# Depthwise convolution of the large groups in 64x64 tiles of TensorE, its output written to DRAM in parts of 48 and 10 partitions

## The chip, the cores and the metric

One core of one Trainium2 chip. The time is the device time of one execution in microseconds (us), lower is better. A run that is compared with the kernel before shares its chip and its rounds with it.

## The reference

The kernel computes a causal depthwise convolution of seven taps over x (8 sequences x 4160 tokens x 192 channels; the taps are a softmax of a weight for each of 8 heads, 24 channels per head), and then a channel mix on its result y:

```python
out = np.einsum('hk,bskhg->bshg', w, x_unf)          # y: 7 taps, 8 heads of 24 channels
xk = mu_k * x + (1.0 - mu_k) * x_prev                # x is now y, x_prev is y one token earlier
xr = mu_r * x + (1.0 - mu_r) * x_prev
k = np.maximum(xk @ w_k, 0.0)                        # 192 -> 1024
v = k * k @ w_v                                      # 1024 -> 192
r = 1.0 / (1.0 + np.exp(-(xr @ w_r)))                # 192 -> 192
return (r * v).astype(np.float32)
```

## The kernel before

The sequences are done in four pairs. TensorE works in bundles: four matmul sections K (`k_mm`, 64 rows x 128 columns of weights, two row halves at a time), one section r of the same shape, one section V of full 128x128 shape, and in most bundles one *unit* of convolution for tokens that are needed later. The convolution is a matmul with a banded Toeplitz matrix per head, `toe`: 128 rows of x (six of them halo) give 120 tokens of y. x is loaded in groups of up to ten such blocks. The first four groups are small and are transposed on TensorE; the large ones (10 and 9 blocks in the first pair, then 10, 10, 10, 5 per pair) are written to DRAM as y and read back by a transposing transfer into yT.

```python
    def conv_mm(g, c):                         # a unit: two chunks, one bank of PSUM each
        ...
        ps2 = ring.tile([P, 2, BANK], FP32, tag="k", name="ps_c")
        for k, hs in enumerate(chunks(g)[c : c + 2]):
            w = G * len(hs)
            ps = ps2[:, k, 0 : nb * 2 * w].rearrange("p (n s c) -> p n s c", n=nb, s=2)
            conv_ps[g, c + k] = ps
            for i, h in enumerate(hs):
                nc.tensor.matmul(out=ps[:, :, :, i * G : (i + 1) * G], lhsT=toe[:, h, :],
                    rhs=xbs[g][:, :nb, :, h * G : (h + 1) * G], start=True, stop=True)
    ...
    def y_write(g):
        ...
        nc.sync.dma_start(
            out=y_drams[p][blk0 * BLK : (blk0 + nb) * BLK, :].rearrange("(n t) c -> t n c", t=BLK),
            in_=ys[g][:BLK, :nb, :])
    ...
    def conv(g, c):
        ...
        conv_mm(g, c)                          # four or two matmuls, then their copies
        for k in range(c, min(c + 2, len(chunks(g)))):
            conv_out(g, k, nc.scalar.copy)
    ...
        for b in range(quads[-1][2] + 1):      # one bundle (cut): K, r, V, then convolution
            k_section(part); k_relu(n); run(rq, b); run(vq, b); run(mixes, b)
            k_square(n); run(vo, b); run(xt, b); run(late, b)
```

PSUM is a ring of four tiles of two banks each; K, r, V, the convolution and the transposes take turns in it. ScalarE does the relus, the sigmoids and the copies of the convolution. VectorE does the squares, the mixes and the final products.

## Time and profile before

| | before |
|---|---|
| median of 4 runs | 436.25 us (436.14 to 436.48) |
| TensorE busy | 421.9 us of 434.0 (97%) |
| bundle with one large unit / without | 6.344 us / 5.937 us |
| from the K section of the second bundle to that of the eighth, six bundles (18.03 to 62.04 us) | 44.01 us |

The bundle lengths are differences of the start times of K sections in the trace; they repeat to 0.001 us through most of the run. The stretch from 18 to 62 us is called the *start stretch* below; it holds the fourth group, then four bundles with the first pair's large groups, two units to a bundle, and one bundle with a single unit.

### The profile page before, as it was taken

To read this page: it belongs to the slowest core of one execution; us is meant where nothing else is said; L and a number is where in the kernel's file an instruction comes from. 1 tells how busy PE (TensorE), PEld (TensorE's weight loads), DVE (VectorE), ACT (ScalarE), POOL (GpSimd) and SP (SyncE) were. 2 spreads that over 40 slices of the span, in tenths; PEclk is the share of its full clock that TensorE was granted. 3 is DMA by queue.
4 is the path that set the end of the run, shared out by engine and by line. 5 is a ranking of instruction groups with operands and counts; after the bars stand their busy time and mean duration, and the time that the engine had idled before them with its cause. 6 is when DMAs were issued, how large, how long until landed. Compare 5 with 4: busy or idle time off the path is not lost.

```text
span 434.0 us, 11361 instructions
## 1 busy us (share of the span) xinstructions
PE 421.9 (97%) x4709; PEld 294.6 (68%) x4709; DVE 380.3 (88%) x678; ACT 349.2 (80%) x474; POOL 48.4 (11%) x73
## 2 busy tenths in 40 slices
PE   8789999999999999999999999999999999999995
PEld 3465767766866776677677667766766776667785
DVE  6879889998988989889888998898898898999983
ACT  5788988888897788889888888888898788777780
POOL 7450001202300000202110100102000000000000
PEclk9999999999999999999999999999999999999999
DMA  8998766999797953869598982696744463621223
GB/s 134 191 153 142 191 174 121 209 200 181 172 170 212 182 149 98 130 178 196 162 167 179 186 170 75 138 227 131 178 118 130 121 159 117 114 68 46 74 74 110
DMA packets 134484, 64.30 MB, mean 148 GB/s; under 512 B 85132, under 2 KB 134048, under 8 KB 134432
## 3 DMA queue, kind: packets, MB, share of 16 engines
q1 hardware_dynamic: 96050, 48.31, 44.8%
q0 software_dynamic: 37488, 14.66, 29.3%
q8 instruction: 37, 0.61, 0.6%
q10 hardware_dynamic: 894, 0.61, 0.5%
q14 instruction: 15, 0.12, 0.1%
HBM read 29.92 MB, written 36.99 MB: 154 GB/s over the span
## 4 chain that ended last, share of the span: by engine, by line
PE 89%; ACT 3%; DVE 3%; DMA 2%; issue 1%; POOL 1%; ACTq 0%
PE ps_v L515 41%; PE ps_k L458 37%; PE ps_r L532 7%; PE ps_c L285 4%; DMA wk<-in_moe_w_k_dram 2%; ACT k_sb L487 2%; ACT y L324 1%; DVE k L501 1%; DVE yT L367 0%; POOL xb L125 0%; PE ps_t L358 0%; DVE xr L434 0%; DVE d L411 0%; DVE xk L438 0%; DVE xk L434 0%
## 5 line engine op out<-in xcount | busy, mean ns | idle before, releaser
L487 ACT ACTIVATE k_sb<-ps_k 128x1024 bf16<-128x1024 f32 x260 | 246.6, 1053 | 25.6 <-PE ps_k L458 25.0
L515 PE MATMUL ps_v<-wv,k 128*128 128x192 bf16 x2080 | 182.7, 246 | 1.3 <-ACT k_sb L487 1.3
L458 PE MATMUL ps_k<-xk,wk 64*128 64x512 bf16 (+1 forms) x1632 | 180.9, 367 | 1.9 <-DVE xk L438 1.0
L515 PEld LDWEIGHTS <-k 128*128 128x128 bf16 x2080 | 168.7, 98 | 11.3 <-issue 11.3
L501 DVE TENSOR_TENSOR k<-k_sb 128x1024 bf16<-128x1024 bf16 x260 | 168.0, 687 | 0.4 <-ACT k_sb L487 0.2
L458 PEld LDWEIGHTS <-wk 64*128 64x128 bf16 x1632 | 74.7, 94 | 97.1 <-issue 19.0
L556 DVE TENSOR_TENSOR o_sb<-ps_v,r_sb 128x768 f32<-128x768 f32 x64 | 61.2, 957 | 35.3 <-PE ps_v L515 33.4
L324 ACT CAST y<-ps_c 120x480 bf16<-120x480 f32 (+4 forms) x134 | 54.3, 483 | 43.7 <-PE ps_c L285 43.7
L540 ACT ACTIVATE r_sb<-ps_r 128x768 bf16<-128x768 f32 x65 | 56.4, 867 | 1.3 <-PE ps_r L532 1.3
L125 POOL DMA_DIRECT2D xb<-in_x_dram x34 | 30.8, 910 | 210.5 <-PE ps_k L458 164.6
L532 PEld LDWEIGHTS <-xr 64*128 64x128 bf16 x780 | 34.1, 94 | 16.8 <-issue 1.4
L532 PE MATMUL ps_r<-wr,xr 64*128 64x192 bf16 x780 | 42.9, 243 | 1.6 <-DVE xb L105 0.8
L434 DVE TENSOR_SCALAR xk<-d,mu 128x512 bf16<-128x512 bf16 (+1 forms) x99 | 33.0, 389 | 1.2
L411 DVE TENSOR_TENSOR d<-yT 128x1536 bf16<-128x1536 bf16 (+2 forms) x35 | 31.1, 888 | 1.3 <-DMA yT<-y_dram 1.2
L438 DVE TENSOR_TENSOR xr<-xr,yT 128x1536 bf16<-128x1536 bf16 (+1 forms) x33 | 31.0, 938 | 1.1
L438 DVE TENSOR_TENSOR xk<-xk,yT 128x1536 bf16<-128x1536 bf16 (+1 forms) x32 | 30.4, 950 | 1.1
L434 DVE TENSOR_SCALAR xr<-d,mu 128x512 bf16<-128x512 bf16 (+1 forms) x102 | 29.1, 341 | 0.0
L285 PE MATMUL ps_c<-xb,toe 128*128 128x480 bf16 (+2 forms) x120 | 28.7, 338 | 0.0
L285 PEld LDWEIGHTS <-toe 128*128 128x128 bf16 x120 | 11.0, 98 | 1.0
L395 POOL COPY y_tail<-yT 128x195 bf16<-128x195 bf16 x4 | 1.7, 434 | 78.5 <-DMA yT<-y_dram 78.5
L651 PE MATMUL warm<-zeros,ones_t 128*128 128x512 bf16 x16 | 6.2, 570 | 1.8 <-DVE zeros L666 1.8
L367 DVE COPY yT<-ps_t 128x720 bf16<-128x720 bf16 (+1 forms) x7 | 3.2, 500 | 4.1 <-PE ps_t L358 4.1
(52 smaller groups left out, 51.2 us busy)
## 6 DMA issues: line engine op xcount, KB each, us to landing
out_dram<-o_sb SPq DMA_DIRECT2D x128, 192.0 KB, 2.4
y_dram<-y SPq DMA_DIRECT2D x10, 900.0 KB, 6.3
xb<-in_x_dram POOLq DMA_DIRECT2D x14, 480.0 KB, 8.7
xb<-in_x_dram POOLq DMA_DIRECT2D x6, 432.0 KB, 6.6
xb<-in_x_dram POOLq DMA_DIRECT2D x10, 192.0 KB, 6.4
y_dram<-y SPq DMA_DIRECT2D x3, 450.0 KB, 3.9
y_dram<-y SPq DMA_DIRECT2D x1, 810.0 KB, 5.6
xb<-in_x_dram POOLq DMA_DIRECT2D x2, 384.0 KB, 7.5
```

What stands on the lines that cost most here:

```text
L285: nc.tensor.matmul(out=ps[:, :, :, i * G : (i + 1) * G], lhsT=toe[:, h, :], rhs=xbs[g][:, :nb, :, h * G : (h + 1) * G], start=True, stop=True,
L324: copy(out=y[:, :, i, :, a - i * Q : b - i * Q], in_=ps[:BLK, :, :, a - c0 : b - c0])
L411: nc.vector.tensor_tensor(out=shaped(s, diffs[s][:, cs, :L]), in0=y_of(s, cs, 1), in1=y_of(s, cs, 0), op=ALU.subtract)
L434: nc.vector.tensor_scalar(out=t[:, c, :L], in0=d[:, c, :L], scalar1=mu[:, i, c : c + 1], scalar2=None, op0=ALU.mult)
L438: nc.vector.tensor_tensor(out=o, in0=o, in1=y_of(s, sl, 0), op=ALU.add)
L458: nc.tensor.matmul(out=ps[:, i, f * L : (f + 1) * L], lhsT=wk[r, c, fs], rhs=xk[r, c, :L], start=c == 0 and f == 0, stop=c == NC - 1 and f ...
L487: nc.scalar.activation(out=k_sb, in_=ps.rearrange("p a b -> p (a b)"), func=AF.Relu)
L501: nc.vector.tensor_tensor(out=o, in0=i, in1=i, op=ALU.mult)
L515: nc.tensor.matmul(out=o, lhsT=k2s[s][:, f, t * P : (t + 1) * P], rhs=wv[:, f, :], start=(f == 0), stop=(f == NF - 1),)
L532: nc.tensor.matmul(out=ps[:, i, k * D : (k + 1) * D], lhsT=xr[q, c, ts], rhs=wr[q, c, :], start=c == 0, stop=c == NC - 1,)
L540: nc.scalar.activation(out=r_sbs[s, j], in_=ps[:, :, 0 : 2 * D], func=AF.Sigmoid)
L556: nc.vector.tensor_tensor(out=o_sb.rearrange("p (b t) d -> p b (t d)", b=2), in0=v_ps.pop((s, j)), in1=r_sbs.pop((s, j)), op=ALU.mult,)
```

## The change

The Toeplitz matrix is a narrow band, so most of a 128x128 matmul multiplies zeros. In 64x64 tiles, 64 rows of x give 58 tokens, and four tiles (two row halves times two column halves) work at once: half of the streamed columns for the same tokens. So a block becomes two half blocks of 58 tokens. Writes go out for each half of the partitions, in parts of 48 and 10, loads come in halves of 64 partitions, the groups get other bounds (10 and 10 blocks in the first pair, whose second group had 9; then 10, 10, 10, 6), and a unit is copied out of PSUM from both banks in one instruction.

```diff
     def conv_mm(g, c):
-        ps2 = ring.tile([P, 2, BANK], FP32, tag="k", name="ps_c")
-        for k, hs in enumerate(chunks(g)[c : c + 2]):
-  ... (one 128x128 matmul per head)
+        ps = ring.tile([P, 2, BANK], FP32, tag="k", name="ps_c")
+        for k, h in enumerate(hs):
+            for j in range(2):
+                for i in range(2):
+                    nc.tensor.matmul(
+                        out=ps[j * Q : (j + 1) * Q, i, 0 : nb * w].rearrange(...)[:, :, :, k * G : (k + 1) * G],
+                        lhsT=toe[i * Q : (i + 1) * Q, h, i * Q : (i + 1) * Q],
+                        rhs=xbs[g][i * Q : (i + 1) * Q, j * nn : (j + 1) * nn, :, h * G : (h + 1) * G],
+                        start=True, stop=True)
+
+    def conv_full(g, c, copy):                 # the fourth group stays 128x128
+        ...
+        for k in range(2):
+            for i in range(2):
+                nc.tensor.matmul(out=ps[:, :, :, i * G : (i + 1) * G], lhsT=toe[:, h, :], ...)
+            for a, b in pieces(c0, c0 + w):
+                copy(out=y[:, :, a // Q, ...], in_=ps[:BLK, :, :, a - c0 : b - c0])
 ...
     def y_write(g):
-        nc.sync.dma_start(out=y_drams[p][blk0 * BLK : (blk0 + nb) * BLK, :].rearrange(...), in_=ys[g][:BLK, :nb, :])
+        for j in range(2):
+            rows = y_drams[p][r0 : r0 + nb * HB, :].rearrange("(n t) c -> t n c", t=HB)
+            for t0, t1 in ((0, HB // 16 * 16), (HB // 16 * 16, HB)):
+                nc.sync.dma_start(out=rows[t0:t1], in_=ys[g][j * Q + t0 : j * Q + t1, :nb, :])
 ...
+        if g == 3:
+            return conv_full(g, c, nc.scalar.copy)
```

More of the change, by code (lines that the diff above doesn't have):

```diff
@@ L38 @@
     BLK = 120
+    HB = 58
     GB = 10
@@ L82 @@
     last_bundle = [bundle_of[st[3] + st[4] - 1] for st in steps]
-    groups = []
+    groups, base = [], []
     for p in range(NPAIR):
@@ L88 @@
         for nb, s, on_pe in (
-            ((3, 0, True), (4, 1, True), (4, 2, True), (5, 3, True), (10, 4, False), (9, 6, False))
+            ((3, 0, True), (4, 1, True), (4, 2, True), (5, 3, True), (10, 4, False), (10, 6, False))
             if p == 0
-            else ((10, 0, False), (10, 2, False), (10, 4, False), (5, 7, False))
+            else ((10, 0, False), (10, 2, False), (10, 4, False), (6, 6, False))
         ):
             groups.append((p, blk0, nb, first_bundle[first_step[p] + s], on_pe))
+            if on_pe:
+                base.append(blk0 * BLK)
+            elif groups[-2][4] or blk0 == 0:
+                base.append(blk0 * BLK)
+            else:
+                base.append(base[-1] + 2 * HB * groups[-2][2])
             blk0 += nb
@@ L107, in x_tile, with load_x_halves @@
             nc.gpsimd.memset(xb[0:32, 0, :, :], 0.0)
-        if blk0 + nb == NBLK:
+        if g > 3 and base[g] + 2 * HB * nb >= S:
             nc.gpsimd.memset(xb[:, nb - 1, :, :], 0.0)
+    def load_x_halves(g):
+        p, _, nb, _, _ = groups[g]
+        xb = xbs[g]
+        for s in range(2):
+            b = 2 * p + s
+            for i in range(2):
+                full = []
+                for m in range(nb):
+                    r0 = base[g] + (2 * m + i) * HB - HALO
+                    lo, hi = max(0, -r0), min(Q, S - r0)
+                    if lo == 0 and hi == Q:
+                        full.append(m)
+                    elif hi > lo:
+                        nc.gpsimd.dma_start(
+                            out=xb[i * Q + lo : i * Q + hi, m, s, :], in_=x[b, r0 + lo : r0 + hi, :]
+                        )
+                nc.gpsimd.dma_start(
+                    out=xb[i * Q : (i + 1) * Q, full[0] : full[-1] + 1, s, :],
+                    in_=bass.AP(
+                        tensor=x.tensor,
+                        offset=x.offset + (b * S + base[g] + (2 * full[0] + i) * HB - HALO) * D,
+                        ap=[[D, Q], [2 * HB * D, len(full)], [1, D]],
+                    ),
+                )
     def load_x(g):
         p, blk0, nb, _, _ = groups[g]
+        if g > 3:
+            return load_x_halves(g)
         xb = xbs[g]
@@ L120, in load_x @@
             t0 = blk0 * BLK - HALO
-            if blk0 + nb == NBLK:
-                hi = nb - 1
-                r0 = t0 + hi * BLK
-                nc.gpsimd.dma_start(out=xb[0 : S - r0, hi, s, :], in_=x[b, r0:S, :])
             nc.gpsimd.dma_start(
@@ L268, with pieces, conv_units @@
     conv_ps = {}
-    def chunks(g):
-        n = max(1, min(3, BANK // (2 * G * groups[g][2])))
+    def pieces(c0, c1):
+        cuts = [c0] + [a for a in range(Q, D, Q) if c0 < a < c1] + [c1]
+        return list(zip(cuts, cuts[1:]))
+    def conv_units(g):
+        n = min(H, BANK // (G * groups[g][2]))
         return [range(h, min(H, h + n)) for h in range(0, H, n)]
@@ L278, in conv_mm @@
             ys[g] = two.tile([P, GB, 2 * D], BF16, tag="y", name="y")
+        ps = ring.tile([P, 2, BANK], FP32, tag="k", name="ps_c")
+        hs = conv_units(g)[c]
+        w = G * len(hs)
+        nn = nb // 2
+        conv_ps[g, c] = ps
+        for k, h in enumerate(hs):
+            for j in range(2):
+                for i in range(2):
+                    nc.tensor.matmul(
+                        out=ps[j * Q : (j + 1) * Q, i, 0 : nb * w].rearrange("p (n s c) -> p n s c", n=nn, s=2)[
+                            :, :, :, k * G : (k + 1) * G
+                        ],
+                        lhsT=toe[i * Q : (i + 1) * Q, h, i * Q : (i + 1) * Q],
+                        rhs=xbs[g][i * Q : (i + 1) * Q, j * nn : (j + 1) * nn, :, h * G : (h + 1) * G],
+                        start=True,
+                        stop=True,
+                    )
+    def conv_full(g, c, copy):
+        nb = groups[g][2]
+        if c == 0:
+            ys[g] = two.tile([P, GB, 2 * D], BF16, tag="y", name="y")
+        y = ys[g][:BLK, :nb, :].rearrange("p n (c s q) -> p n c s q", c=NC, s=2)
         ps2 = ring.tile([P, 2, BANK], FP32, tag="k", name="ps_c")
-        for k, hs in enumerate(chunks(g)[c : c + 2]):
-            w = G * len(hs)
+        w = 2 * G
+        for k in range(2):
             ps = ps2[:, k, 0 : nb * 2 * w].rearrange("p (n s c) -> p n s c", n=nb, s=2)
-            conv_ps[g, c + k] = ps
-            for i, h in enumerate(hs):
+            for i in range(2):
+                h = 4 * c + 2 * k + i
                 nc.tensor.matmul(
@@ L290, in conv_mm @@
                     stop=True,
+                )
+            c0 = (4 * c + 2 * k) * G
+            for a, b in pieces(c0, c0 + w):
+                copy(
+                    out=y[:, :, a // Q, :, a % Q : a % Q + b - a], in_=ps[:BLK, :, :, a - c0 : b - c0]
                 )
@@ L315, in conv_out @@
         nb = groups[g][2]
-        hs = chunks(g)[c]
+        hs = conv_units(g)[c]
         ps = conv_ps.pop((g, c))
-        y = ys[g][:BLK, :nb, :].rearrange("p n (c s q) -> p n c s q", c=NC, s=2)
         c0, c1 = hs[0] * G, hs[-1] * G + G
-        a = c0
-        while a < c1:
-            i = a // Q
-            b = min(c1, (i + 1) * Q)
-            copy(out=y[:, :, i, :, a - i * Q : b - i * Q], in_=ps[:BLK, :, :, a - c0 : b - c0])
-            a = b
+        src = ps[:, :, 0 : nb * (c1 - c0)].rearrange("p i (n s c) -> p i n s c", n=nb // 2, s=2)
+        y = ys[g][:, :nb, :].rearrange("p (n i) (c s q) -> p i n c s q", i=2, c=NC, s=2)
+        for a, b in pieces(c0, c1):
+            copy(out=y[:, :, :, a // Q, :, a % Q : a % Q + b - a], in_=src[:, :, :, :, a - c0 : b - c0])
     def new_yT(p):
         yTs[p] = two.tile([P, 3, -(-(YC + NBLK * BLK) // 16) * 16], BF16, tag="yT", name="yT")
-        y_drams[p] = dram.tile([NBLK * BLK, 2 * D], BF16, tag=f"y{p % 2}", name="y_dram")
+        y_drams[p] = dram.tile([S + 2 * P, 2 * D], BF16, tag=f"y{p % 2}", name="y_dram")
         nc.vector.memset(yTs[p][:, :, 0:YC], 0.0)
@@ L336, in y_write @@
             new_yT(p)
-        nc.sync.dma_start(
-            out=y_drams[p][blk0 * BLK : (blk0 + nb) * BLK, :].rearrange("(n t) c -> t n c", t=BLK),
-            in_=ys[g][:BLK, :nb, :],
-        )
+        for j in range(2):
+            r0 = base[g] + j * nb * HB
+            rows = y_drams[p][r0 : r0 + nb * HB, :].rearrange("(n t) c -> t n c", t=HB)
+            for t0, t1 in ((0, HB // 16 * 16), (HB // 16 * 16, HB)):
+                nc.sync.dma_start(out=rows[t0:t1], in_=ys[g][j * Q + t0 : j * Q + t1, :nb, :])
     def y_read(g):
         p, blk0, nb, _, _ = groups[g]
-        r0, r1 = blk0 * BLK, min((blk0 + nb) * BLK, S)
+        r0 = base[g] // 16 * 16
+        r1 = min((base[g] + 2 * nb * HB) // 16 * 16, S)
         nc.sync.dma_start_transpose(
@@ L596, in conv @@
             return conv_small(g, (act_, act_, dve_ if g == 0 else act_))
+        if g == 3:
+            return conv_full(g, c, nc.scalar.copy)
         conv_mm(g, c)
-        for k in range(c, min(c + 2, len(chunks(g)))):
-            conv_out(g, k, nc.scalar.copy)
+        conv_out(g, c, nc.scalar.copy)
     for g, (p, blk0, nb, fb, on_pe) in enumerate(groups):
-        nx = 1 if g < 3 else -(-len(chunks(g)) // 2)
+        nx = len(conv_units(g))
         if g == 0:
@@ L611 @@
         for i, b in enumerate(xs):
-            at(xt, b, conv, g, 2 * i)
+            at(xt, b, conv, g, i)
         if on_pe:
```

## The prediction

> **What bounds the kernel now.** I read the page first: the engine table, then the chain that ended last, then the costliest groups. These are its lines.
>
> ```profile
> PE 421.9 (97%) x4709; PEld 294.6 (68%) x4709; DVE 380.3 (88%) x678; ACT 349.2 (80%) x474; POOL 48.4 (11%) x73
> ...
> PE 89%; ACT 3%; DVE 3%; DMA 2%; issue 1%; POOL 1%; ACTq 0%
> PE ps_v L515 41%; PE ps_k L458 37%; PE ps_r L532 7%; PE ps_c L285 4%; DMA wk<-in_moe_w_k_dram 2%; ACT k_sb L487 2%; ACT y L324 1%; DVE k L501 1%; DVE yT L367 0%; POOL xb L125 0%; PE ps_t L358 0%; DVE xr L434 0%; DVE d L411 0%; DVE xk L438 0%; DVE xk L434 0%
> ...
> L324 ACT CAST y<-ps_c 120x480 bf16<-120x480 f32 (+4 forms) x134 | 54.3, 483 | 43.7 <-PE ps_c L285 43.7
> ...
> L285 PE MATMUL ps_c<-xb,toe 128*128 128x480 bf16 (+2 forms) x120 | 28.7, 338 | 0.0
> ```
>
> TensorE is the bound: 97% busy and 89% of the chain. The convolution of the large groups (L285) is 4% of the chain. ScalarE's copies of its results (L324) wait 43.7 us for TensorE, not the other way round. Busy time of matmuls overlaps, so for costs I use start times in the timeline of TensorE around 191 us (one bundle with convolution) and around 132 us (one without).
>
> ```profile
> 190.80 0.66 PE L532 MATMUL ps_r<-wr,xr 64*128 64x192 bf16 x12
> 191.39 2.81 PE L515 MATMUL ps_v<-wv,k 128*128 128x192 bf16 x32
> 194.04 0.57 PE L285 MATMUL ps_c<-xb,toe 128*128 128x480 bf16 x2
> 194.54 2.77 PE L458 MATMUL ps_k<-xk,wk 64*128 64x512 bf16 x24
> 197.14 0.66 PE L532 MATMUL ps_r<-wr,xr 64*128 64x192 bf16 x12
> 197.73 2.81 PE L515 MATMUL ps_v<-wv,k 128*128 128x192 bf16 x32
> 200.38 0.57 PE L285 MATMUL ps_c<-xb,toe 128*128 128x480 bf16 x2
> 200.88 2.76 PE L458 MATMUL ps_k<-xk,wk 64*128 64x512 bf16 x24
> ```
>
> ```profile
> 131.84 2.76 PE L458 MATMUL ps_k<-xk,wk 64*128 64x512 bf16 x24
> 134.44 0.66 PE L532 MATMUL ps_r<-wr,xr 64*128 64x192 bf16 x12
> 135.03 2.81 PE L515 MATMUL ps_v<-wv,k 128*128 128x192 bf16 x32
> 137.78 0.60 PE L458 MATMUL ps_k<-xk,wk 64*128 64x512 bf16 x4
> ```
>
> With convolution the bundle runs from 194.54 to 200.88, 6.34 us; without it from 131.84 to 137.78, 5.94 us. No idle time is noted on any line. So **one unit of convolution (two heads of 480 columns) costs TensorE 0.40 us**, 0.20 per matmul, all of it on the path. Next, the change of tile shape. V matmuls of 192 columns take (194.04 - 191.39)/32 = 83 ns. The r matmuls are also 192 columns, in pairs on two 64-row tiles; six pairs at 83 ns would take 0.50 us, but V starts 0.59 us after them. K after convolution starts 0.50 us after it, 0.40 of which are the two matmuls. V to K without convolution is 2.75, with 2.65 for V itself. Each time about **0.10 us goes where the shape changes** (64x128 to 128x128 and back). K to r (same shape) is 2.60 for 12 pairs of 512 columns, 217 ns each: no loss. V to convolution (both 128x128) has none either.
>
> [...] The trace has weight loads of 128 columns only (94 ns with 64 rows, 98 with 128[...])[...].
>
> **The change part by part.**
> - *Removed.* By the instruction order, before has 40 units of 2x480 columns, 4 of 2x432 (the second large group of the first pair) and 6 of 4x240 (the 5-block groups). At 0.407, 0.366 and 0.41 us (0.407 is the same bundle difference by more starts): 16.3 + 1.5 + 2.5 = **20.2 us** of TensorE on the path. This is an upper bound for any gain on TensorE.
> - *Added.* A head becomes four matmuls of 240 columns on four 64x64 tiles, so a quad takes one tile's time if all four run together: half of 0.204, 0.102 us. After has 44 units of two quads (ten blocks) and nine units for the three 6-block groups, 24 quads of 144 columns at 0.061 us. Sum: 88 x 0.102 + 24 x 0.061 = **10.4 us**.
> - *Added: a change of shape.* The unit stands between V (128x128) and K (64x128). Before, V to convolution was free; now both sides change. One more change per unit: 53 x 0.10 = **5.3 us**.
> - [...]
> - *TensorE's net*: 20.2 - 10.4 - 5.3 - 1.3 = **3.2 us gained**.
> - *ScalarE.* It copies two heads from two banks in one instruction of 128x960 instead of two of 120x480. From 480 (570 ns), 768 (867) and 1024 (1053) elements, 960 is about 1.0 us, against 1.14. Three copies of 480, 320 and 160 (570, 447, 311) become two of 320 and 640 (447 and about 710). Per 10-block group 4.9 us become about 4.3. In the steady part this is off the path. At 41 to 56 us, with two units a bundle, the bundles take some 7 us and V waits 0.23 us for ScalarE each time; there I count **0.4 us** gained.
> - *Transfers.* Each large write becomes four, the loads twice as many of half the partitions, with some 3% more rows (64 read per 58 kept instead of 128 per 120). Writes landed in 6.3 us, transposing reads in 7.5, and from the second pair on a read is issued some four bundles before its first use, so nothing of this is on the path. One place is tight: the read of the first large group makes VectorE wait 1.2 us at 57.6 us, with K following at 62.0. If three more issues at about 0.45 us (the median of these) delay it by 1 us, some 0.5 us of slack is left. I count nothing.
>
> **The rivals.**
> - *Weight loads become the bound.* [...] Against it: the two row halves load in parallel (r pairs at 83 ns with two 94 ns loads each). For it: column tiles are new here.
> - *No exposed loads, cheap change*: without the 1.3 us the time is about 431.3.
> - *Another engine takes over.* VectorE is busy 45 of each 50 us; bundles of 6.2 us instead of 6.34 leave it room (bundles of 5.94 run without TensorE waiting). ScalarE gets less work. Unlikely.
> - *A late transfer in the first pair* (write in four parts, then the transposing read): TensorE would wait before the bundle near 62 us, 1 to 2 us at most, once.
>
> **Range and chances.** 436.2 - 3.2 - 0.4 = **432.6 us**. The low end, 430.6, is free weight loads and a fully used ScalarE gain; the high end, 436.8, is column-serial loads or a startup stall. More than 2% faster (under 427.5) would need more than 8.7 of the 9.8 us that remain when quads run at full speed and the change of shape is free: 0.02. More than 2% slower needs serial loads: 0.04. The rest, 0.94, is within 2%.
>
> **What would show it.** In the timeline after, bundles with a large unit should take 6.2 to 6.27 us instead of 6.34, those without still 5.94. V to convolution should gain some 0.10 us between the last V matmul and the first of the quad. The four matmuls of a quad should start within some 20 ns of one another, and the next quad about 0.10 us later[...]. TensorE should stay at 97% and nothing should wait for the writes. The prediction is wrong if quads do not run together, if the shape change costs much more than 0.10 us for 64x64 tiles, or if a wait for yT or xb appears on TensorE's chain.

One term of the sum: 1.3 us lost (25 ns for each of 53 units, for weight loads that nothing hides), a guess of mine that I had not worked out from a trace. The sum is 20.2 - 10.4 - 5.3 - 1.3 = 3.2 us gained on TensorE and 0.4 on ScalarE, so 436.2 - 3.2 - 0.4 = 432.6 us; the terms that stand alone give 4.5 and 0.4 us, and 431.3 us.

## More of the kernel before

Other lines of the page are in the prediction. One more is needed later: the clock that was granted to TensorE, in tenths, for 40 slices of the span.

```profile
PEclk9999999999999999999999999999999999999999
```

## The result

The changed kernel takes 434.80 us (median of 4 runs, 433.62 to 435.05) against 436.25 us. The ratio is 0.9961, with a 95% interval of 0.9942 to 0.9979. All ratios here are the mean time of one kernel's fast runs over that of the other's fast runs of the same rounds, so they are not quite the ratio of the medians. The gain is 1.5 us by the medians and 1.7 us by the ratio, where 3.6 us had been predicted.

These are lines of the page after: the engines, the clock row, the chain by line, ScalarE's copies and the 64x64 weight loads.

```profile
PE 419.2 (97%) x5045; PEld 293.3 (68%) x5045; DVE 377.2 (87%) x678; ACT 348.0 (80%) x427; POOL 62.5 (14%) x101
...
PEclk9989999999999999999999999999999999999999
...
PE ps_v L576 41%; PE ps_k L519 38%; PE ps_r L593 7%; PE ps_c L321 4%; ACT k_sb L548 3%; DMA wk<-in_moe_w_k_dram 2%; ACT y L384 1%; POOL xb L155 0%; ACT y L351 0%; PE ps_c L342 0%; PE ps_t L419 0%; ACT r_sb L601 0%; PE ps_c L366 0%; POOL wk L214 0%; DVE x_f L720 0%
...
L384 ACT CAST y<-ps_c 128x960 bf16<-128x960 f32 (+7 forms) x81 | 50.7, 668 | 45.4 <-PE ps_c L321 45.4
...
L321 PEld LDWEIGHTS <-toe 64*64 64x64 bf16 x448 | 8.3, 105 | 7.7 <-issue 7.7
```

TensorE is still the bound. A 64x64 weight load is recorded with 105 ns; those of 128 columns have 94 ns (64 rows) and 98 (128 rows). Two things are new on the page: an 8 in the clock row in the third slice, and two lines of the old 128x128 path with ScalarE (`ACT y L351`, `PE ps_c L342`) in the chain. Both are in the first 33 us. The steady part first, in TensorE's timeline (start, length, engine, line, operation):

```profile
188.70 0.40 PE L321 MATMUL ps_c<-xb,toe 64*64 64x240 bf16 x8
189.03 2.76 PE L519 MATMUL ps_k<-xk,wk 64*128 64x512 bf16 x24
...
194.97 0.40 PE L321 MATMUL ps_c<-xb,toe 64*64 64x240 bf16 x8
195.30 0.39 PE L519 MATMUL ps_k<-xk,wk 64*128 64x512 bf16 x2
```

The bundle is 195.30 - 189.03 = 6.27 us (6.267 by more digits of the start times), against 6.344; the prediction's terms, the guess of 0.025 among them, give 5.937 + 0.204 + 0.10 + 0.025 = 6.27. In the single records the four weight loads of a quad start within 10 ns, its matmuls too, and the second quad starts 126 ns after the first. From the K section at 64.11 us to the last one, the changed kernel takes 352.61 us; the same stretch before takes 355.26 us. **The steady part gained 2.65 us.** The prediction's terms for it, with that guess, come to 2.6 us.

So the rest is at the start. The start stretch (18.77 to 64.11 us) takes 45.34 us instead of 44.01: **1.33 us lost**, where the prediction had counted about 0.9 us gained. (The stretch itself began at 18.77 instead of 18.03 us. In the profiles here it begins at 17.8 to 18.5 us in the kernels built on the one before and at 18.3 to 18.9 us in those built on the changed one. I leave this out; that the change adds nothing there is not shown.) TensorE's timeline of the fourth group, first the kernel before, then the changed one:

```profile
22.87 1.09 PE L285 MATMUL ps_c<-xb,toe 128*128 128x240 bf16 x8
24.09 2.79 PE L458 MATMUL ps_k<-xk,wk 64*128 64x512 bf16 x24
```

```profile
23.61 0.37 PE L342 MATMUL ps_c<-xb,toe 128*128 128x240 bf16 x2
25.09 0.57 PE L342 MATMUL ps_c<-xb,toe 128*128 128x240 bf16 x4 [1.10 <-ACT y L351]
26.69 0.56 PE L342 MATMUL ps_c<-xb,toe 128*128 128x240 bf16 x2 [1.03 <-ACT y L351]
27.18 4.07 PE L519 MATMUL ps_k<-xk,wk 64*128 64x512 bf16 x24
```

Before, eight matmuls run in one go. After, they come as two, a wait of 1.10 us for ScalarE's copy, four, a wait of 1.03 us, and two. This is the new `conv_full`: matmuls of the first bank, their copies, matmuls of the second bank, their copies. Both banks are one PSUM tile, and in the program as built the second pair waits for the copies of the first. Before, all four matmuls of a unit were issued ahead of the copies. And then the K section takes 4.07 us instead of 2.79: inside it, pairs that take 216 ns elsewhere start 427 ns apart until 29.7 us. The windows from 25 to 30 us show why (window, its length, busy time and instructions per engine, granted clock, share of DMA time, GB/s), before and after:

```profile
25.00:30.00 5.00, 3.66 (x45) 2.22 (x42) 3.89 (x8) 4.47 (x8) 1.37 (x3) 1.00 1.51 181
```

```profile
25.00:30.00 5.00, 3.88 (x21) 1.54 (x21) 4.13 (x9) 2.81 (x8) 1.57 (x4) 0.66 1.59 189
```

The granted clock is 0.66 on average there: the clock record holds 0.5 for 3.4 us, from 26.4 to 29.9 us. In the 3.4 us before it (23.0 to 26.4 us) TensorE was busy for 1.55 us and never waited longer than 1.10 us. What sets such a spell off is not shown here: e1_order and e12_no_copy both wait 1.12, 0.24 and 0.60 us for ScalarE between 27 and 31 us, and the V section after that takes 2.80 us in e1_order and 4.44 in e12, at a granted clock of 0.66 from 30 to 35 us. So waits of 2.1 us were followed by a spell at half clock in which K alone took 1.3 us longer.

### The profile page after: what moved, and what is told of

Same layout as the page of the kernel before. It is cut to its first block, busy times and chain, and to the rows that moved or that the text cites. A ratio compares the mean times of both kernels' runs of the same rounds, so it can differ in the third digit from the quotient of the medians.

```text
span 433.3 us, 12070 instructions
## 1 busy us (share of the span) xinstructions
PE 419.2 (97%) x5045; PEld 293.3 (68%) x5045; DVE 377.2 (87%) x678; ACT 348.0 (80%) x427; POOL 62.5 (14%) x101
## 4 chain that ended last, share of the span: by engine, by line
PE 90%; ACT 4%; DMA 2%; issue 2%; POOL 1%; DVE 0%; ACTq 0%
PE ps_v L576 41%; PE ps_k L519 38%; PE ps_r L593 7%; PE ps_c L321 4%; ACT k_sb L548 3%; DMA wk<-in_moe_w_k_dram 2%; ACT y L384 1%; POOL xb L155 0%; ACT y L351 0%; PE ps_c L342 0%; PE ps_t L419 0%; ACT r_sb L601 0%; PE ps_c L366 0%; POOL wk L214 0%; DVE x_f L720 0%
## 5 line engine op out<-in xcount | busy, mean ns | idle before, releaser
L384 ACT CAST y<-ps_c 128x960 bf16<-128x960 f32 (+7 forms) x81 | 50.7, 668 | 45.4 <-PE ps_c L321 45.4
L134 POOL DMA_DIRECT2D xb<-in_x_dram x56 | 40.3, 732 | 205.5 <-PE ps_k L519 158.8
L495 DVE TENSOR_SCALAR xk<-d,mu 128x512 bf16<-128x512 bf16 (+1 forms) x99 | 30.3, 361 | 1.2
L321 PE MATMUL ps_c<-xb,toe 64*64 64x240 bf16 (+1 forms) x448 | 20.0, 265 | 0.0
L321 PEld LDWEIGHTS <-toe 64*64 64x64 bf16 x448 | 8.3, 105 | 7.7 <-issue 7.7
L131 POOL DMA_DIRECT2D xb<-in_x_dram x14 | 7.6, 544 | 1.4 <-POOL xb L114 0.9
```

The source lines that it names most:

```text
L134: nc.gpsimd.dma_start(out=xb[i * Q : (i + 1) * Q, full[0] : full[-1] + 1, s, :], in_=bass.AP(tensor=x.tensor, offset=x.offset + (b * S + b ...
L321: nc.tensor.matmul(out=ps[j * Q : (j + 1) * Q, i, 0 : nb * w].rearrange("p (n s c) -> p n s c", n=nn, s=2)[:, :, :, k * G : (k + 1) * G], ...
L384: copy(out=y[:, :, :, a // Q, :, a % Q : a % Q + b - a], in_=src[:, :, :, :, a - c0 : b - c0])
L495: nc.vector.tensor_scalar(out=t[:, c, :L], in0=d[:, c, :L], scalar1=mu[:, i, c : c + 1], scalar2=None, op0=ALU.mult)
```

## The experiments

The theory: the steady part is as predicted, and the start lost it through the order of matmuls and copies in the fourth group. The rivals: the transfers in parts, or chance. Then the price of the unit itself is tested, and whether it can be had without the extra change of shape. In this table "stretch" is the start stretch, "bundle" a steady bundle with one 10-block unit, both from the profiled run; "clock" is the mean granted clock of that run. The ratios are to the kernel before in the same rounds; its medians there were 436.27 (e1 to e4), 436.16 (e5 to e7) and 436.03 us (e8 to e11), of 11 runs each. e12_no_copy, with a wrong output, is left out of the table: one run, of unknown state, 433.86 us.

| run | median us | ratio to before (95%) | stretch | bundle | clock |
|---|---|---|---|---|---|
| before | 436.25 | 1 | 44.01 | 6.344 | 1.000 |
| the change | 434.80 | 0.9961 (0.9942 to 0.9979) | 45.34 | 6.267 | 0.995 |
| e1_order | 433.44 | 0.9927 (0.9909 to 0.9945) | 43.76 | 6.267 | 0.997 |
| e2_before_interleaved | 438.06 | 1.0032 (1.0014 to 1.0050) | 45.91 | 6.344 | 0.996 |
| e3_write58 | 528.23 | 1.2081 (1.2040 to 1.2122) | - | - | 0.929 |
| e4_before_parts | 436.13 | 0.9992 (0.9971 to 1.0013) | 44.09 | 6.344 | 0.997 |
| e5_switch128 | 445.22 | 1.0214 (1.0187 to 1.0242) | 44.96 | 6.506 | 1.000 |
| e6_tiny64 | 438.03 | 1.0029 (1.0004 to 1.0053) | 43.92 | 6.299 | 0.999 |
| e7_dve_first | 433.97 | 0.9953 (0.9932 to 0.9974) | 43.77 | 6.267 | 0.997 |
| e8_kr64 (median of all six; of the five fast ones 431.20) | 431.45 | 0.9888 (0.9840 to 0.9937) | 45.30 | 6.160 | 0.993 |
| e11_before_kr64 | 437.10 | 1.0023 (1.0001 to 1.0046) | 44.03 | 6.360 | 0.999 |
| e9_yread | 433.32 | 0.9931 (0.9913 to 0.9950) | 43.76 | 6.267 | 0.998 |
| e10_both | 428.87 | 0.9830 (0.9809 to 0.9851) | 43.67 | 6.160 | 0.997 |

### e1_order: the old order in the changed kernel

```diff
         for k in range(2):
             ... (two matmuls into bank k)
+        for k in range(2):
             for a, b in pieces(c0, c0 + w):
                 copy(...)
```

> The changed kernel with one thing put back: the fourth group (5 blocks, 128x128) issues its four matmuls of a unit first and copies afterwards, as before, instead of matmul pair, copy, matmul pair, copy. Theory A (TensorE waits for ScalarE's copy between the two halves of a PSUM tile, 2.1 us in the trace of the changed kernel, and the bundle at 18 us grew from 6.06 to 8.40 us): the two waits go, that bundle is back near 6.1 us, and the time falls by 1.5 to 2.5 us, to about 432.8. Rival B (the first pair lost time to transfers in more parts, or the start merely varies): time as the changed kernel's, 434.8 +- 0.5. Steady bundles stay 6.267 us under both.

The output is right. TensorE's timeline of the fourth group:

```profile
23.36 0.99 PE L342 MATMUL ps_c<-xb,toe 128*128 128x240 bf16 x8
24.37 2.79 PE L521 MATMUL ps_k<-xk,wk 64*128 64x512 bf16 x24
```

Eight matmuls in one go again, K in 2.79 us, no spell at half clock in the record until the kernel's last few us, and the stretch falls from 45.34 to 43.76 us. The bundle expected near 6.1 us took 5.85. The median is 433.44 us: 1.4 us gained by the medians, a little less than the 1.5 to 2.5 expected.

### e2_before_interleaved: the new order in the kernel before

```diff
+            if g == 3:
+                conv_out(g, c + k, nc.scalar.copy)     # straight after the two matmuls of chunk k
```

> The kernel before with only this order put in: its fourth group copies each half straight after its matmuls. Theory A: the bundle at 18 us grows by some 2 us with waits of TensorE for ScalarE, time 436.2 + 1.5 to 2.5 = about 438. Rival B: 436.2, no change. Steady bundles stay 6.344 us.

The same loss appears in the kernel that has nothing else of the change. The waits of this run (who waited for whom, us in total, times, longest):

```profile
PE ps_c L285 <- ACT y L326: 2.3, 2, 1.3
```

The stretch is 45.91 us instead of 44.01, the bundle at 18 us 8.40 instead of 6.06, and the clock record has 0.5 for 3.4 us from 27.2 us on. The mean clock was 0.995 or 0.996 in all six of this kernel's runs. In the changed kernel it was so in three of four runs; the fourth, at 0.998, was its fastest (433.62 us). In e1_order it was 0.997 to 1.000. Rival B is refuted by both runs: the order costs 1.4 to 1.8 us, forwards and backwards. How this splits between the waits and the spell is not shown. The one run of the changed kernel at 0.998 is only 0.2 us above e1's median, which speaks for the spell; and the kernel before, without this order, had 3 of its 11 runs in these rounds at 0.993 to 0.996, and they took 437.7 to 438.2 us. So the order makes the spell usual, but is not its only cause.

### e4_before_parts: the transfers alone

```diff
-        nc.sync.dma_start(out=..., in_=ys[g][:BLK, :nb, :])
+        for t0, t1 in ((0, 48), (48, 58), (58, 106), (106, BLK)):
+            nc.sync.dma_start(out=rows[t0:t1], in_=ys[g][t0:t1, :nb, :])
```

(and each large load of x in two halves of 64 partitions)

> The kernel before with the transfers alone changed: each large write in four parts of 48, 10, 48 and 14 partitions, each large load of x in two of 64 partitions; convolution and copies as before. Theory A (these are hidden everywhere): 436.2 +- 0.4, bundles of the first pair as before. Rival B (the parts cost the first pair about 1 us): 437 to 438, with VectorE's wait for yT at 57 us grown beyond 1.2 us or a wait for xb.

Theory A holds: ratio 0.9992, stretch 44.09 us. Cutting the transfers costs nothing that can be measured here.

### e3_write58: no cut at 48

```diff
-            for t0, t1 in ((0, HB // 16 * 16), (HB // 16 * 16, HB)):
+            for t0, t1 in ((0, HB),):
```

> e1_order with each half written in one transfer of 58 partitions instead of 48 and 10. [...]VectorE and then TensorE wait for yT from the first large group on, and the time rises by tens of us, 450 to 550. Rival: the cut is harmless, landing stays near 6 us and the time is e1_order's within 0.5 us.

The first large write is issued at 45.1 us, and the read that has to wait for it at 66.6 us, instead of 50.2 us in e1_order. VectorE's and then TensorE's timeline of this run:

```profile
72.23 0.96 DVE L474 TENSOR_TENSOR d<-yT 128x1536 bf16<-128x1536 bf16 x1 [13.94 <-DMA yT<-y_dram]
```

```profile
75.16 1.46 PE L521 MATMUL ps_k<-xk,wk 64*128 64x512 bf16 x6 [11.17 <-DVE xk L501]
```

The time is 528 us. So the cut into 48 and 10 is what makes halves of 58 tokens usable: it removes some 95 us and is not a gain by itself. The reason for expecting so late a write was an estimate of mine: how many DMA engines a transfer of 58 partitions gets is not shown, as no view names them. What the windows show is the share of DMA time and the GB/s (the last two numbers) while a large write ran, in e3 and then in e1_order:

```profile
46.00:54.00 8.00, 7.48 (x100) 5.44 (x98) 6.96 (x13) 7.30 (x10) 0.00 (x0) 1.00 0.13 44
```

```profile
46.00:48.00 2.00, 2.00 (x26) 1.87 (x23) 1.32 (x3) 1.78 (x3) 0.00 (x0) 1.00 0.87 205
```

So while the writes of 58 partitions ran, the core's DMA share was 0.13 at 44 GB/s; with 48 and 10 it was 0.87 at 205 GB/s. SyncE's queue was held as well: by its timeline the issues of the two halves take 8.2 us together, where e1_order's four parts take 3.1, and those of the two outputs behind them another 11.2, until 64.5 us. So the read came late in part because the queue reached it late.

### e5_switch128 and e6_tiny64: the price of a change of shape

```diff
         for k, h in enumerate(hs):
+            if k == 1:   # e5: one 128x128 matmul of 16 columns into unused PSUM; e6: four 64x64 ones
+                nc.tensor.matmul(out=ps[:, 0, BANK - 16 : BANK], lhsT=toe[:, h, :], rhs=xbs[g][:, 0, 0, 0:16], ...)
```

> e1_order with one matmul of 128x128 shape and 16 columns put between the first and the second quad of every large unit (its result goes to unused PSUM columns; the output stays right). Theory: each change of tile shape costs TensorE about 0.093 us and the exposed 64-column weight load 0.024 us. Two more changes and one more exposed load per unit[...]: 0.22 to 0.25 us per unit, a bundle of 6.267 becomes about 6.50, and 53 units cost about 12 us (the steady 45 units 10 us). Rival (the 0.12 us per unit of the changed kernel is not the change of shape but slow column tiles): about +0.03 us per unit as in e6_tiny64.

> The control for e5_switch128: at the same place four matmuls of 64x64 shape and 16 columns, one per tile, so the shape does not change. Theory: only the issue and a weight load that hides less well, 0.02 to 0.07 us per unit, bundle 6.29 to 6.34, time +1 to +3.5 us over e1_order. [...]

The prices in these expectations are from the changed kernel's trace: a quad starts 0.176 us after the last V matmul where V matmuls are 0.083 apart, so 0.093 for the change of shape; the second quad starts 0.126 us after the first where its columns were put at 0.102, so 0.024, which I put down to a weight load that nothing hides.

TensorE's timeline of e5, then of e6:

```profile
192.42 0.30 PE L329 MATMUL ps_c<-xb,toe 64*64 64x240 bf16 x4
192.65 0.18 PE L320 MATMUL ps_c<-xb,toe 128*128 128x16 bf16 x1
192.77 0.30 PE L329 MATMUL ps_c<-xb,toe 64*64 64x240 bf16 x4
193.00 0.39 PE L529 MATMUL ps_k<-xk,wk 64*128 64x512 bf16 x2
```

```profile
191.01 0.30 PE L331 MATMUL ps_c<-xb,toe 64*64 64x240 bf16 x4
191.13 0.18 PE L322 MATMUL ps_c<-xb,toe 64*64 64x16 bf16 x4
191.16 0.28 PE L331 MATMUL ps_c<-xb,toe 64*64 64x240 bf16 x4
```

With the same number of streamed columns, a matmul of another shape adds 0.239 us to the bundle (6.506 - 6.267), four of the same shape 0.032 us. Less some 0.03 us for the matmul (e6's 0.032) and 0.02 for the exposed load (the 0.024 above), two changes of shape cost 0.19 us, close to 0.095 each (an estimate). e5's 445.2 us is 11.8 us above e1_order, as expected. Serial weight loads are refuted: e6 adds four more loads for 0.032 us, and one load of 64 columns is recorded with 105 ns in the changed kernel. e6's time (438.0 us) is worse than its bundles tell and misses the expected +1 to +3.5 us: its profile has a wait of VectorE for yT, which e9 takes up.

```profile
DVE d L484 <- DMA yT<-y_dram: 4.2, 1, 4.2
```

### e7_dve_first and e12_no_copy: what bounds the start stretch

```diff
-        conv_out(g, c, nc.scalar.copy)
+        conv_out(g, c, nc.vector.tensor_copy if g < 6 and c % 2 else nc.scalar.copy)   # e7
```

(e12: GpSimd writes zeros in place of those copies; the output is wrong)

> e1_order with VectorE instead of ScalarE copying every second unit of the two large groups of the first pair. Theory (the bundles of some 6.95 us from 43 to 64 us, with two units each, are bound by ScalarE: copies 1.75 us, then the relus that V waits for): half of the copies leave ScalarE, about 0.9 us per bundle, and these four bundles shorten to between 6.5 and 6.7 us: 1 to 1.8 us gained in all against e1_order. Rival (VectorE is as full, its squares come late): no change or slower, with waits for VectorE in their place.

> Wrong output on purpose. e1_order in which every second unit of the two large groups of the first pair is not copied by anyone: GpSimd writes zeros in its place. This takes some 0.9 us of copying per two-unit bundle from ScalarE and gives VectorE nothing. If ScalarE's copies and relus set the length of the bundles at 41 to 62 us (6.96, 6.96 and 6.76 us in e1_order), they fall to what TensorE needs for two units, 5.94 + 2 x 0.33 = about 6.6 us or 6.45 [...]. If VectorE or TensorE sets them, they stay at 6.9 or above. Only these bundles are read; the time may shift by about 1 us for reasons of start and transfers.

The reason for e12's second figure, 6.45 us: a second unit, which follows one of its own shape, would pay for no change of shape. That was an estimate; e12's two-unit bundle from 49.87 us, which has no wait, takes 6.47 us.

In e1_order the four bundles from 34 to 62 us (the last has one unit, the others two) take 7.31, 6.96, 6.96 and 6.76 us. In e8 TensorE has 0.1 us less to do between convolution and K, and they take 7.33, 6.96, 6.96 and 6.76: this work is not on the path. In e5 it has nearly 0.5 us more in a two-unit bundle, and they grow by 0.24 in three cases and not at all in the last. So about one unit's extra time, of two, reaches the length: TensorE alone does not set them. Where V waits in e1_order, in TensorE's timeline:

```profile
45.30 2.80 PE L578 MATMUL ps_v<-wv,k 128*128 128x192 bf16 x32 [0.24 <-ACT k_sb L550]
48.03 0.60 PE L321 MATMUL ps_c<-xb,toe 64*64 64x240 bf16 x16
48.56 2.76 PE L521 MATMUL ps_k<-xk,wk 64*128 64x512 bf16 x24
```

With half of the copies gone (e12) they take 6.55, 7.00, 6.47 and 6.27 us, 1.7 us less together, and V no longer waits for ScalarE: three of four come to within 0.1 us of what TensorE needs. In its timeline the V section after 52 us, with no wait:

```profile
52.47 0.66 PE L598 MATMUL ps_r<-wr,xr 64*128 64x192 bf16 x12
53.06 2.82 PE L581 MATMUL ps_v<-wv,k 128*128 128x192 bf16 x32
```

So the chain through ScalarE's copies and relus sets these bundles. With the copies moved to VectorE (e7) they take 7.13, 7.48, 7.12 and 6.27 us, no gain in sum, and TensorE waits in another place:

```profile
43.16 2.12 PE L521 MATMUL ps_k<-xk,wk 64*128 64x512 bf16 x18 [0.83 <-DVE o_sb L619]
```

VectorE is the next bound, close behind. My expectation for e7 failed. (e12's total says nothing: its run had a spell at half clock at 31 us, before these bundles, and it was run once.)

### e8_kr64 and e11_before_kr64: one change of shape less

```diff
+                for h in range(2):
                     for i in range(2):
                         nc.tensor.matmul(
-                            out=ps[:, i, f * L : (f + 1) * L], lhsT=wk[r, c, fs],
+                            out=ps[h * Q : (h + 1) * Q, i, f * L : (f + 1) * L],
+                            lhsT=wk[r, c, fs.start + h * Q : fs.start + (h + 1) * Q],
```

(and the same for r)

> e1_order with K and r in 64x64 tiles as well (each 64x128 pair becomes a quad of the same streamed columns). If the 0.12 us that a unit pays besides its columns is the change of tile shape, then from convolution to K there is no change any more: 2 changes per bundle instead of 3, bundle 6.267 - 0.09 = about 6.17 us, bundles without convolution 5.937 + 0.024 = about 5.96 (V to K still changes, its first weight load is now the slow one), time 433.4 - 45 x 0.09 + 13 x 0.024 = about 429.7. Rival (the price belongs to the convolution's own tiles, or the 64-column weight loads bind K and r): bundles 6.27 or longer.

> Control: the kernel before with K and r in 64x64 tiles, convolution in 128x128 as it was. The number of shape changes per bundle stays 2, so the theory expects no gain: bundles 6.344 + 0.024 = about 6.37, without convolution 5.96, time 436.2 + 64 x 0.024 = about 437.8. If K and r are faster in 64x64 tiles by themselves, bundles fall below 6.34.

TensorE's timeline of e8:

```profile
181.26 0.40 PE L321 MATMUL ps_c<-xb,toe 64*64 64x240 bf16 x8
181.49 2.76 PE L522 MATMUL ps_k<-xk,wk 64*64 64x512 bf16 x48
184.08 0.67 PE L597 MATMUL ps_r<-wr,xr 64*64 64x192 bf16 x24
```

K starts 0.23 us after the convolution instead of 0.33, takes 2.59 us as before although it has twice the matmuls, and the bundle is 6.160 us: 0.107 less. Bundles without convolution grow from 5.937 to 5.956. The control has no change of shape to save and loses 0.017 us, 6.360 against 6.344, which I put down to its first 64-column load. Both agree with the theory to 0.02 us. e8's median of 431.45 us is above the expected 429.7, because its runs scatter: 429.2 to 435.5 us (a sixth, 436.45, is slow and left out of the ratio). Its profiled run, 431.2 us, has a spell at half clock at 31 us (its mean clock is 0.993) and a bundle of 6.74 us at 89 us; its two fastest runs, 429.2 us, are near the expectation.

### e9_yread and e10_both: the scatter, and the candidate

```diff
-            at(late, xs[-1] + (1 if g == 4 else 2), y_read, g)
+            at(late, xs[-1] + (1 if g < 6 else 2), y_read, g)
```

> e1_order with the transposing read of the second large group of the first pair issued one bundle earlier, before the loads of x at 70 us instead of together with them. In e1_order's profile the bundle at 87 us is 0.35 us long of that read, in e6_tiny64's two bundles 3.6 us. Expected: no bundle above 6.30 us between 64 and 145 us, and 0.3 to 1 us gained on the median of e1_order (433.4), with less spread between runs. Rival (the late read is chance and unrelated to the loads): a wait for yT of the same size shows up again.

> e8_kr64 and e9_yread together, as the candidate that beats both kernels: about 429.2 us if both work and do not collide; VectorE (87% busy) has less room in bundles of 6.17 us, so up to 1 us may be given back in waits for VectorE.

e9's profile has no bundle above 6.30 us from 64 to 145 us. The median is only 0.1 us below e1_order's, which ran on another chip, not the 0.3 to 1 expected, and by the ratios there is no gain (0.9931 and 0.9927); but the runs lie between 433.12 and 433.38 us instead of 433.12 and 434.16. With both, the time is 428.87 us (428.52 to 429.14, 4 runs), ratio 0.9830: the best version here, with a right output. A profile each cannot tell how often the late read strikes. That its cause is the issue together with the loads of x at 70 us is not shown: it is gone in e9's one profile, but the changed kernel's own profile has the read at 72.19 and the loads at 72.27 us, and no wait. e10's profile still has a bundle of 6.46 us at 93 us, without a wait for yT.

## Why the prediction was right or wrong

- **TensorE is the bound, and quads run at half the columns' time: right.** The four tiles start within 10 ns, and from quads of 144 columns to quads of 240 the step to the next quad grows from 0.087 to 0.126 us, 0.41 ns a column; one 128x128 matmul of 480 columns takes 0.202 us, 0.42 ns a column.
- **One more change of shape at 0.10 us: right.** e5 and e6 give about 0.095, e8 gains 0.107 by leaving one out.
- **0.025 us for the exposed load: the size right, by luck.** It was chosen, not derived. The time appears ahead of the second quad, one step later than I had placed it: it starts 0.126 us after the first, not 0.102 (with 144 columns 0.087, not 0.061). A load of 64 columns is recorded with 105 ns. e11 shows 0.017 for K's. That these 0.017 to 0.024 us are a load that nothing hides is my reading; no run takes it apart.
- **The steady part: right.** 2.65 us measured, 2.6 by the terms.
- **The first pair: the step that failed.** Its terms were some 0.5 us of TensorE's net for the nine units of the start stretch and 0.4 us of ScalarE's, together 0.9 us gained; it lost 1.33. Two things are in this. First, the part-by-part list did not see that the fourth group, which keeps its shape, had its matmuls and copies put in another order. That cost 1.6 us of the stretch (45.34 to 43.76 in e1): two waits of 1.1 us for ScalarE, and a spell at half clock after them. Second, the rest of the first pair gained 0.25 us (44.01 to 43.76 in e1), not 0.9. ScalarE sets its bundles, so TensorE's gain there is hidden. And ScalarE's gain was mis-sized: I added the durations of single copies (4.9 us a group to 4.3), but neighbouring instructions overlap. The copies of a two-unit bundle of the first large group, and the relus that follow them, before and after:

```profile
41.10 2.01 ACT L324 CAST y<-ps_c 120x480 bf16<-120x480 f32 x5 [1.10 <-PE ps_c L285]
42.96 3.83 ACT L487 ACTIVATE k_sb<-ps_k 128x1024 bf16<-128x1024 f32 x4
```

```profile
43.35 1.88 ACT L384 CAST y<-ps_c 128x640 bf16<-128x640 f32 x3 [1.04 <-PE ps_c L321]
45.11 3.81 ACT L548 ACTIVATE k_sb<-ps_k 128x1024 bf16<-128x1024 f32 x4
```

  From start to start that is 1.86 us before and 1.76 after: 0.1 us gained. In the second large group, which grew from 9 to 10 blocks, it is 1.71 before and 1.76 after: nothing gained. Over the four bundles ScalarE gained some 0.1 us, not 0.4.
- **The rivals.** Serial or column-serial weight loads: refuted (four loads start within 10 ns, and e6's four more add 0.032 us). Another engine takes over: not in the steady part, but ScalarE already held the start, which the prediction had seen in V's waits of 0.23 us without taking TensorE's gain out of the sum there. A late transfer in the first pair: it exists in five later profiles (e1, e6, e7, e8, e12), but at the second large group's read, near 84 us, and not at the first one's, where I had looked. The changed kernel's own profile does not have it, so it is no part of the loss above.

## What to carry to other kernels

Read an order listing for the parts that a change is *not* about: a copy put between two matmuls of one PSUM tile cost as much as half of what the change gained (1.4 us by e1, 1.8 by e2, where the steady part gained 2.65). Count the changes of TensorE's tile shape per round of the loop; if a neighbouring section can take the same shape at no cost in streamed columns, a change of shape disappears (here 0.107 us a bundle in e8, and 4.4 us of 433, e9 to e10). Where a stage waits for another engine, take the gain of the faster engine out of the sum of that stage.
